# Frequency-pair layout for the scratch tensors of a two-stage transform in a gated convolution kernel

## The chip, the cores and the metric

The kernel runs on one core of a Trainium2 chip. The metric is the device time of one execution in microseconds; lower is better. A core has a matrix engine (PE, with its weight loads PEld), a vector engine (DVE), a scalar engine (ACT), a general engine (POOL) and a synchronisation engine (SP). SP issues most of the transfers between device memory (DRAM) and the on-chip memory; ACT and POOL issue some. The transfers themselves are carried out by 16 DMA engines that all issuers share.

## The reference

The input `x` has 2048 tokens of 512 channels. Two branches are mixed by a gate:

```python
g = sigmoid((x * gate_w).sum(-1))                        # one gate per token
K[d, l] = Re(sum_n C[d,n] * exp(dt[d]*A[d,n]*l) * dt[d]*B[d,n])   # 2048 taps per channel, complex A, B, C
a = irfft(rfft(pad(x)) * rfft(pad(K)))[:2048] + x * Dskip # causal convolution over the tokens
b = gelu(x @ w1 + b1) @ w2 + b2                           # 512 -> 1792 -> 512
out = g * a + (1 - g) * b
```

Everything is float32.

## The kernel before

The program has two halves in time. The function `front` runs the dense branch `b`, the making of the taps `K`, and the first stage of the transform of both `x` and `K`. The function `conv` then runs the second stage of both transforms, their product, the inverse transform, and the mix with the gate.

**The transform in two stages.** The tokens are split into 64 slots of 32 tokens. `first_stage` (L405) multiplies one slot's 32 rows by a constant matrix `c1` of 32 x 64, which gives 32 frequencies, each with a real and an imaginary part: 64 partitions, 512 channels. One call handles eight slots. Signal results are copied to on-chip tiles by ACT and stored by SP into the DRAM scratch tensor `tu_d` (L437, one store of 64 partitions and 128 KB per slot). Tap results are gathered in the tiles `sk` (two of them, each used again two calls later) and stored into `tk_d` (L802, 64 stores of 128 KB, each 64 partitions times 16 slots times 32 channels, so in pieces of 128 bytes).

Both scratch tensors have the shape [32 frequencies, 128, 512]; the 128 are the two parts times the 64 slots. So what the second stage needs of one frequency lies in one piece of 256 KB, in the order in which it stands on the 128 partitions of the chip, and the stores have the stride.

**The second stage.** `conv` walks over 16 pairs `s` of frequencies, `n = 2s` and `n = 2s+1`. Per pair, `signal(s)` and `taps(s)` multiply the loaded tiles `us[n]` and `t2s[n]` by 128 x 64 matrices (L1188), the two frequencies of the pair side by side. `product(s)` multiplies the results on DVE (L1210 to L1215), `inverse(s)` transforms back on PE (L1227), and `turn(s)` copies the two results on ACT into two of six tiles `sa` (L1239) and stores them with SP into a third scratch tensor `t4_d` (L1241). A tile `sa` is used again three pairs later, so its copy then waits until the store has landed. After the 16 pairs the last matrices (L1343) and the gate give the result.

**The loads.** The 32 tiles of the signal are loaded from `tu_d`: 27 of them by `early` in `front` (L462), as soon as rooms on the chip come free, and 5 in `conv` (L1307, for `s` of 4 to 6). The 32 tiles of the taps are loaded by `fetch` (L1167): 16 ahead of the first pair, then four in each of the pairs 0 to 3. Eight of these tiles lie in the pool `tk` and are used twice, 16 in the tile `t3`.

**The order.** In `front` the order of every instruction is a list written into the program (`ORDER`, L89), made from estimated costs and due times; it fixes the order on each engine's queue and SP's too. In `conv` the order is that of the Python loop (L1283 to L1328). SP issues its transfers strictly in that order: one that waits holds back all behind it. Completion is counted on eight semaphores that are taken in turn, and a transfer waits for the eighth transfer before it on SP, so SP has at most eight under way.

**The result.** It is kept as [16 token tiles, 128, 512]. In `front` the dense branch is written to it (L1032) and, for the second half of the hidden columns, added to it in memory from POOL (L1038). In `conv` it is read back two tiles at a time by `mix` (L1266), and stored two tiles at a time (L1362), the last two singly (L1360).

Of the kernel before, what the change touches and what calls it, by code (L numbers as in the profile page):

```python
# [9 lines left out]
F32 = mybir.dt.float32  # L10
# [4 lines left out]
ALU = mybir.AluOpType  # L15
# [3 lines left out]
P = 128  # L19
L = 2048  # L20
D = 512
# [61 lines left out]
N_ATTIC, N_LOFT, N_TK = 11, 8, 8  # L83
# [75 lines left out]
    return [32 + m if m < 32 else 63 - m for m in range(64)]  # L159


def k0_order():
    return [8 * (n % 4) + n // 4 for n in range(32)]

# [15 lines left out]
def constants():  # L180


    def om(e4):
        a = 2.0 * np.pi * (np.asarray(e4) % (4 * L)) / (4 * L)
        return np.cos(a), -np.sin(a)

    k0 = np.arange(32)
    p = np.arange(32)
    q = np.asarray(slot_q())
    k1 = np.arange(64)  # L190
    m = np.arange(32)

    er, ei = om(4 * (64 * np.outer(p, k0) + 16 * p[:, None]))

    c1 = np.tile(np.stack([er, ei], 2).reshape(32, 64), (4, 1))
    some = np.arange(P)[:, None] == np.arange(P) // 4
    c1 = np.concatenate([c1, some], 1)


    ko = np.asarray(k0_order())  # L200
    turn = 2.0 * np.pi * (ko[:, None] + 0.25) / 32
    half = 2.0 * np.pi * (ko[:, None] + 0.25) / 64
    g1 = np.zeros((P, 2, 2, 32))
    for b in range(2):
        up, down = turn * (p - 1), turn * p
        if b:
            rows = [np.cos(up), -np.sin(up), -np.sin(up), -np.cos(up)]
            rows += [np.cos(down), -np.sin(down), np.sin(down), np.cos(down)]
        else:
            z = np.zeros_like(up)  # L210
            rows = [np.cos(down), -np.sin(down), z, z]
            rows += [z, z, np.cos(up + half), -np.sin(up + half)]
        for sign in range(2):
            for kind, c in ((0, 0), (0, 1), (1, 0), (1, 1)):
                a = rows[4 * sign + 2 * kind + c] / L
                for n in range(32):
                    g1[seat(n, c, kind), b, sign] = a[n]
    g1 = g1.reshape(P, 128)


    f2 = np.zeros((32, 2, 64, 64))
    g2 = np.zeros((32, 64, 32, 2))
    for n, k in enumerate(ko):
        er, ei = om(4 * np.outer(q - 31.5, k + 32 * k1) + (q - 31.5)[:, None])
        f2[n, 0], f2[n, 1] = er, -ei
        a = 2.0 * np.pi * (k + 32 * k1 + 0.25) / L
        g2[n, :, :, 0] = np.cos(np.outer(a, m))
        g2[n, :, :, 1] = np.sin(np.outer(a, m))
        g2[n, :, 0, 1] = 1 - 2 * (k1 % 2)
    f2 = f2.reshape(8, 4, P, 64).transpose(0, 2, 1, 3).reshape(8, P, 256)  # L230
    g2 = g2.reshape(8, 2, P, 64).transpose(0, 2, 1, 3).reshape(8, P, 128)
    c2 = np.concatenate([f2, g2], 2)
    return (
        np.ascontiguousarray(c1, dtype=np.float32),
        np.ascontiguousarray(g1, dtype=np.float32),
        np.ascontiguousarray(c2, dtype=np.float32),
    )
# [38 lines left out]
def gated_mix(  # L276
# [18 lines left out]
    nc = tc.nc  # L295
# [3 lines left out]

    dt_d = dr.tile([1, D], F32, name="dt_d")  # L300
    t4_d = dr.tile([4, 2, GROUP, 2, 32, D], F32, name="t4_d")
    tu_d = dr.tile([32, P, D], F32, name="tu_d")
    tk_d = dr.tile([32, P, D], F32, name="tk_d")

    half_pi = cp.tile([P, 1], F32, name="half_pi")
    nc.vector.memset(half_pi, PI / 2)
# [22 lines left out]
    def front(pool, psum, keep, attic, loft, den, pr):  # L329
# [89 lines left out]
            for r, (bank, key) in enumerate(banks):  # L419
                evac(r, bank, key)  # L420

        rows = tu_d.rearrange("k (c t) d -> (k c) t d", c=2)

        def signal():
            for s in range(8):
# [18 lines left out]
        def early():  # L444

            us = places(attic, loft, den)
            keys = [("ux", 0)] + [("st", k) for k in range(3)]
            keys = [*keys, *(("ld", k) for k in range(N_LD)), "gwb"]
            yield 1e6
            cc, f1 = first(pr)  # L450
            move(192, lambda: nc.sync.dma_start(cc, c2[0]), T_EARLY, [], ["pr"])
            act(0.6, lambda: parted(cc, f1), T_EARLY, [], ["pr"])
            for n in range(N_US):
                m = n - N_DEN
                if m < 0:
                    due, key = T_DEN + n, [("xc", n // 4)]
                elif m < N_ATTIC:
                    due, key = T_EARLY + 2.5 * m, [keys[m]]
                else:
                    due, key = T_LOFT + m, ["xt", "xv"] if m < N_ATTIC + 4 else ["tt"]  # L460
                move(
                    256, lambda n=n: nc.sync.dma_start(us[n], tu_d[k0_order()[n]]), due,  # L462
                    [("u_d", k) for k in range(64)], key,
                )
            yield None
# [285 lines left out]
        def contract(u, c, k, t):  # L751
# [45 lines left out]
            for h in range(8):  # L797
                n, ss = h % 2, slice(h // 2 * 16, h // 2 * 16 + 16)
                d = u * UW + n * 64 + c // 2 * 32

                def store(n=n, ss=ss, d=d):
                    nc.sync.dma_start(  # L802
                        tk_d[:, :, d : d + 32].rearrange("k (c s) g -> (k c) s g", c=2)[:, ss],
                        sk[half][64 * n : 64 * n + 64, ss].rearrange("p s j g -> p s (j g)"),
                    )

                move(300, store, t + 5, [("sk", half, j) for j in range(4)], [], hold=1.4)
# [180 lines left out]
        def output(i, t):  # L988
# [18 lines left out]
            for s in range(2):  # L1007
                if b == NB - 1 and s >= 2 - N_LATE:
                    for n, f in enumerate(fs):
                        late.append((s, hi[:, n], lo[:, n], wh[1][f % FH], wl[1][f % FH]))  # L1010
                    continue
                q = (2 * b + s) % N_ACC
                n = 3 * len(fs)
                if b == NB - 2 and j == 3:
                    late.append((2 + s, hi[:, 0], lo[:, 0], wh[1][fs[0] % FH], wl[1][fs[0] % FH]))
                else:
                    mm(
                        0.2305 * n, lambda s=s, q=q: products(s, acc[q]), t + LAG + D_OUT * (j == 3),
                        [hk, lk, *ws], [("acc", q)],
                    )  # L1020
                if j == 3:
                    n = b % NSB * 2 + s
                    r = (2 * b + s) % 2
                    act(
                        0.58, lambda n=n, q=q, r=r: nc.scalar.mul(io[r], acc[q], gate[:, 1, n : n + 1]),
                        t + D_EV, [("acc", q), ("gate", b % NSB)], [("io", r)],
                    )
                    if b + 1 < NSB:
                        seed(q, t + D_EV)
                    if b < NSB:  # L1030
                        move(
                            256, lambda n=n, r=r: nc.sync.dma_start(out[n], io[r]), t,  # L1032
                            [("io", r)], [("v", n)],
                        )
                    else:
                        move(
                            512,
                            lambda n=n, r=r: nc.gpsimd.dma_start(out[n], io[r], accum_op=ALU.add),  # L1038
                            t, [("io", r)], [("v", n)], queue="GP",
                        )  # L1040

# [106 lines left out]
    def conv(pool, ps, late, attic, loft, den, pr):  # L1148
# [10 lines left out]
            nc.sync.dma_start(cc, c2[m])  # L1159
            c4s[m] = cc  # L1160

        def fetch(n):
            if N_TK <= n < N_TK + 16:
                t2s[n] = t3[:, 16 + n - N_TK if n < N_TK + 8 else n - N_TK]
            else:
                t2s[n] = pool.tile([P, D], F32, tag="tk", name=f"tk{n}", bufs=N_TK)
            nc.sync.dma_start(t2s[n], tk_d[ko[n]])  # L1167

        def matrices(m):

# [87 lines left out]
        def mix(k, on):  # L1258
# [4 lines left out]
            else:  # L1263
                r -= N_ATTIC
                mos[k] = loft[:, r * D : (r + 2) * D].rearrange("p (s d) -> p s d", s=2)
            on.dma_start(mos[k], out[2 * k : 2 * k + 2].rearrange("s p d -> p s d"))  # L1266

        def rest(n):

# [10 lines left out]
                nc.tensor.matmul(accs[s], l[:, ss], w, start=False, stop=last)  # L1280
                n -= 1

        for n in range(N_TK):  # L1283
            if n == 4:
                factors(1)
            fetch(n)
            if n == 1:
                t3 = pool.tile([P, 24, D], F32, name="t3", bufs=1)
                g1t = pool.tile([P, 2, 64], F32, name="g1t", bufs=1)
        for n in range(N_TK, N_TK + 8):  # L1290
            fetch(n)
        nc.sync.dma_start(g1t, g1.rearrange("p (b k) -> p b k", b=2))
        matrices(0)
        signal(0)
# [4 lines left out]
        for s in range(16):  # L1299

            if s % 2 or s == 0:
                if s < 10:
                    factors((s + 5) // 2)
            for n in range(16 + 4 * s, 20 + 4 * s) if s < 4 else ():
                fetch(n)
            for n in range(2 * s + N_ROOM, min(2 * s + N_ROOM + 2, 32)) if s > 3 else ():
                nc.sync.dma_start(us[n], tu_d[ko[n]])  # L1307
            product(s)
            if 1 < s + 1 < 16:
                signal(s + 1)  # L1310
# [22 lines left out]
        for m in range(8):  # L1333
            tag = "pa" if m % 3 == 2 else f"pu{m % 3}"
            for i in range(2):
# [19 lines left out]
                for h, cs in enumerate(parts):  # L1355
# [1 line left out]
                        z[:, cs], pb[:, cs], gate[:, 0, t : t + 1], z[:, cs], ALU.mult, ALU.add  # L1357
                    )
                    if m == 7:
                        (nc.sync, nc.scalar, nc.sync)[i + h].dma_start(out[t][:, cs], z[:, cs])  # L1360
            if m < 7:
                nc.sync.dma_start(out[2 * m : 2 * m + 2].rearrange("s p d -> p s d"), mos[m])  # L1362

    ctx.enter_context(tc.manual_schedule())
    keep = ctx.enter_context(tc.tile_pool(name="keep", bufs=1))
# [78 lines left out]
```

## Time and profile before

| | |
|---|---|
| Median of three runs (lowest to highest) | 492.07 us (490.47 to 492.58) |
| The profiled execution, its own time | 491.67 us |
| Its span, first to last instruction | 489.9 us |
| PE busy | 472.9 us, 97% of the span |
| DVE, ACT, POOL busy | 84%, 74%, 7% |
| Moved by DMA | 107.56 MB, mean 220 GB/s |

The profile's page lists, per engine, the time in which it was busy. "The chain that ended last" is followed back from the last instruction, at each step to what released it. The groups of transfers give the destination and source, the issuing engine, the number, the size of each and the median time from issue to landing. In the view of stages (a row per stretch of time) each engine has its busy time, followed by the clock granted to PE, the mean busy share of the 16 DMA engines and what they moved per second; the share can be a little over 1, since one engine can have two packets open. SPq and ACTq stand for the transfers that these engines issue, and the time of such a row is that of the issue.

### The profile page before, as it was taken

The numbers are of one execution on the slowest core, as the hardware profiler recorded it, in microseconds if no ns is written. First come the engines' busy times: TensorE is split into PE (matmuls) and PEld (weight loads), VectorE is DVE, ScalarE is ACT, GpSimd is POOL, SyncE is SP. The second block draws the span as 40 slices with busy tenths as digits, with TensorE's granted clock in tenths as the row PEclk, the third lists the DMA queues.
The fourth block names the chain that finished last, engine by engine and source line by source line (L and its number), as shares of the span: only waits on it lengthen the run. The fifth ranks groups of instructions, "written<-read, shape, count | busy, mean of one in ns | idle before, by whom it ended". The sixth has DMA issues, their size and how long they took to land.

```text
span 489.9 us, 11986 instructions
## 1 busy us (share of the span) xinstructions
PE 472.9 (97%) x4802; PEld 355.2 (72%) x4802; DVE 413.8 (84%) x645; ACT 363.6 (74%) x660; POOL 36.5 (7%) x63
## 2 busy tenths in 40 slices
PE   9999999997899998999999999999999999999994
PEld 7999878787688787887888878988989322222541
DVE  5879999998999999999999998999921398778355
ACT  6899895889897989999978995769754455655210
POOL 2000000000000000000011011102000100241000
PEclk8999999999899999999999999999999999999998
DMA  8868394920788458967783884884889999979897
GB/s 294 256 225 283 96 311 142 298 95 1 206 238 181 123 166 219 266 162 237 169 212 57 144 183 112 155 219 57 193 209 229 339 374 369 356 281 414 276 332 301
DMA packets 114848, 107.56 MB, mean 220 GB/s; under 512 B 72564, under 2 KB 77064, under 8 KB 114248
## 3 DMA queue, kind: packets, MB, share of 16 engines
q1 hardware_dynamic: 108072, 82.81, 57.3%
q0 software_dynamic: 6016, 20.70, 15.7%
q10 hardware_dynamic: 704, 3.28, 1.9%
q8 instruction: 38, 0.62, 0.5%
q14 instruction: 18, 0.15, 0.1%
HBM read 61.14 MB, written 45.62 MB: 218 GB/s over the span
## 4 chain that ended last, share of the span: by engine, by line
PE 80%; DVE 8%; ACT 7%; issue 2%; DMA 1%; SPq 0%; DVEq 0%; POOL 0%; POOLq 0%
PE ph L957 9%; PE ph L959 9%; PE acc L1000 9%; PE ph L958 9%; PE acc L1001 8%; PE acc L1003 8%; PE pk L761 6%; PE p2u L1188 5%; PE p2k L1188 5%; PE pa L1227 3%; PE ph L416 3%; PE pb L1343 2%; DVE loft L693 1%; DMA t<-tk_d 1%; DVE den L700 1%
## 5 line engine op out<-in xcount | busy, mean ns | idle before, releaser
L957 PE MATMUL ph<-xh,wh 128*128 128x256 f32 x448 | 128.6, 287 | 1.4 <-DVE hl L984 1.4
L959 PE MATMUL ph<-xh,wl 128*128 128x256 f32 x448 | 127.5, 285 | 0.3 <-issue 0.3
L958 PE MATMUL ph<-xlo,wh 128*128 128x256 f32 x448 | 127.4, 284 | 0.0
L957 PEld LDWEIGHTS ph<-xh,wh 128*128 128x128 f32 x448 | 85.8, 192 | 9.9 <-issue 4.1
L958 PEld LDWEIGHTS ph<-xlo,wh 128*128 128x128 f32 x448 | 85.9, 192 | 1.8
L959 PEld LDWEIGHTS ph<-xh,wl 128*128 128x128 f32 x448 | 85.9, 192 | 0.5 <-issue 0.5
L1000 PE MATMUL acc<-wh,hh 128*128 128x512 f32 x208 | 83.8, 403 | 1.0 <-ACT hh L977 0.9
L1003 PE MATMUL acc<-wh,hl 128*128 128x512 f32 x208 | 81.6, 392 | 1.9 <-DVE hl L984 1.9
L1001 PE MATMUL acc<-wl,hh 128*128 128x512 f32 x208 | 81.6, 392 | 0.0
L693 DVE TENSOR_TENSOR loft<-den,wz 128x512 f32<-128x512 f32 (+2 forms) x48 | 67.0, 1396 | 1.2 <-ACT den L675 1.1
L974 ACT ACTIVATE ph<-ph,b1t 128x256 f32<-128x256 f32 x112 | 50.5, 451 | 19.0 <-PE ph L959 17.0
L984 DVE TENSOR_TENSOR hl<-ph,hh 128x512 fp32r<-128x512 f32 (+1 forms) x62 | 38.1, 616 | 23.5 <-ACT hh L977 23.3
L1000 PEld LDWEIGHTS acc<-wh,hh 128*128 128x128 f32 x208 | 39.1, 188 | 15.8 <-issue 4.9
L1003 PEld LDWEIGHTS acc<-wh,hl 128*128 128x128 f32 x208 | 39.1, 188 | 11.7 <-DVE hl L984 3.1
L1001 PEld LDWEIGHTS acc<-wl,hh 128*128 128x128 f32 x208 | 39.1, 188 | 6.0
L1196 ACT COPY k<-p2k 128x512 f32<-128x512 f32 x32 | 18.5, 586 | 26.3 <-issue 10.2
L724 DVE TENSOR_TENSOR y<-y,ea 128x256 f32<-128x256 f32 (+2 forms) x48 | 37.1, 774 | 0.4 <-ACT y L712 0.2
L977 ACT CAST hh<-ph 128x512 fp32r<-128x512 f32 (+1 forms) x62 | 33.0, 532 | 5.9 <-PE acc L1001 1.5
L700 DVE TENSOR_TENSOR den<-loft 128x256 f32<-128x256 f32 (+2 forms) x48 | 37.1, 773 | 0.1
L761 PEld LDWEIGHTS pk<-y,den 128*32 128x32 f32 x2048 | 32.3, 112 | 6.7 <-ACT attic L434 2.8
L736 DVE TENSOR_TENSOR y<-y,loft 128x2048 f32<-128x2048 f32 x16 | 36.6, 2286 | 0.6 <-ACT loft L667 0.5
L761 PE MATMUL pk<-y,den 128*32 128x64 f32 x2048 | 35.1, 226 | 0.8 <-ACT attic L434 0.6
(194 smaller groups left out, 830.2 us busy)
## 6 DMA issues: line engine op xcount, KB each, us to landing
tk_d<-sk SPq DMA_DIRECT2D x64, 128.0 KB, 4.4
t_d<-sa SPq DMA_DIRECT2D x32, 256.0 KB, 5.0
tu_d<-attic SPq DMA_DIRECT2D x48, 128.0 KB, 3.8
attic<-in_xt_dram SPq DMA_DIRECT2D x16, 256.0 KB, 4.5
attic<-in_xs_dram SPq DMA_DIRECT2D x16, 256.0 KB, 4.7
xh_d<-xh SPq DMA_DIRECT2D x8, 512.0 KB, 5.6
xl_d<-xlo SPq DMA_DIRECT2D x8, 512.0 KB, 6.1
out_dram<-io SPq DMA_DIRECT2D x16, 256.0 KB, 3.6
```

The costliest lines, as they stand in the source:

```text
L693: v.tensor_mul(s.rearrange("p (a n l) -> p a n l", n=n, l=CL), a, w.to_broadcast([P, 4 * CH, n, CL]))
L700: v.tensor_add(to, z[:, :, 0], z[:, :, 1])
L761: nc.tensor.matmul(pks[q][32 * j : 32 * j + 32, :, gg], x[:, r, ch // CL, :, ch % CL], y[:, r, ch // CL, :, ch % CL], start=(r == 0), stop ...
L957: nc.tensor.matmul(p, h, xh[xk][:, d], start=(d == 0), stop=False)
L958: nc.tensor.matmul(p, h, xlo[xk][:, d], start=False, stop=False)
L959: nc.tensor.matmul(p, lo, xh[xk][:, d], start=False, stop=(d == 3))
L974: nc.scalar.activation(phs[q][:, n], phs[q][:, n], AF.Gelu_apprx_tanh, bias=b1t[:, f : f + 1])
L984: nc.vector.tensor_sub(lo, phs[q][:, 0:nf], hi.bitcast(F32))
L1000: nc.tensor.matmul(a, h, wh[1][w], start=start, stop=False, skip_group_check=seeded)
L1001: nc.tensor.matmul(a, h, wl[1][w], start=False, stop=False, skip_group_check=seeded)
L1003: nc.tensor.matmul(a, l, wh[1][w], start=False, stop=stop, skip_group_check=seeded)
L1188: nc.tensor.matmul(out[64 * i : 64 * i + 64], w, x, start=True, stop=True)
```

## The change

Four things change in the layout of data in DRAM. Arithmetic, the list `ORDER`, the instructions of PE, DVE and ACT stay the same.

- Both scratch tensors get the shape [64 slots, 16 pairs, 2 parts, 2 of the pair, 512], and the columns of `c1` are put in the order pair, part, member, so that the 64 partitions of a first-stage result stand in the order of the memory. A store of one slot of the signal then fills one piece of 128 KB. A store of the taps keeps its 128-byte pieces, with another stride.
- A signal load (still 256 KB, one frequency) reads its 128 rows of 2 KB through `turned`: parts outermost, then slots, 128 KB apart.
- A tap load brings both frequencies of a pair in one transfer of 512 KB, 16 in place of 32, with rows of 4 KB: again parts outermost, then slots, 128 KB apart.
- The result has the shape [8 pairs of token tiles, 128, 2, 512]; a pair of tiles is one row of 4 KB per partition. The rows that `front` writes singly are 2 KB, 4 KB apart. The host puts the result back in order, outside the measured time.

```diff
+def turned(z, n):
+    return z[:, n // 2, :, n % 2].rearrange("t c d -> c t d")
...
-    c1 = np.tile(np.stack([er, ei], 2).reshape(32, 64), (4, 1))
+    c1 = np.stack([er, ei], 1)[:, :, k0_order()].reshape(32, 2, 16, 2)
+    c1 = np.tile(c1.transpose(0, 2, 1, 3).reshape(32, 64), (4, 1))
...
-    tu_d = dr.tile([32, P, D], F32, name="tu_d")
-    tk_d = dr.tile([32, P, D], F32, name="tk_d")
+    tu_d = dr.tile([64, 16, 2, 2, D], F32, name="tu_d")
+    tk_d = dr.tile([64, 16, 2, 2, D], F32, name="tk_d")
...
-        rows = tu_d.rearrange("k (c t) d -> (k c) t d", c=2)
+        rows = tu_d.rearrange("t s c a d -> (s c a) t d")
...
-                    256, lambda n=n: nc.sync.dma_start(us[n], tu_d[k0_order()[n]]), due,
+                    256, lambda n=n: nc.sync.dma_start(us[n], turned(tu_d, n)), due,
...
-                        tk_d[:, :, d : d + 32].rearrange("k (c s) g -> (k c) s g", c=2)[:, ss],
+                        tk_d[ss, :, :, :, d : d + 32].rearrange("t s c a g -> (s c a) t g"),
...
-                            256, lambda n=n, r=r: nc.sync.dma_start(out[n], io[r]), t,
+                            256, lambda n=n, r=r: nc.sync.dma_start(out[n // 2, :, n % 2], io[r]), t,
...
-                            lambda n=n, r=r: nc.gpsimd.dma_start(out[n], io[r], accum_op=ALU.add),
+                            lambda n=n, r=r: nc.gpsimd.dma_start(out[n // 2, :, n % 2], io[r], accum_op=ALU.add),
...
-        def fetch(n):
+        def fetch(s):
+            n = 2 * s
             if N_TK <= n < N_TK + 16:
-                t2s[n] = t3[:, 16 + n - N_TK if n < N_TK + 8 else n - N_TK]
+                r = 16 + n - N_TK if n < N_TK + 8 else n - N_TK
+                t = t3[:, r : r + 2]
             else:
-                t2s[n] = pool.tile([P, D], F32, tag="tk", name=f"tk{n}", bufs=N_TK)
-            nc.sync.dma_start(t2s[n], tk_d[ko[n]])
+                t = pool.tile([P, 2, D], F32, tag="tk", name=f"tk{s}", bufs=N_TK // 2)
+            t2s[n], t2s[n + 1] = t[:, 0], t[:, 1]
+            nc.sync.dma_start(t, tk_d[:, s].rearrange("t c a d -> c t a d"))
...
-            on.dma_start(mos[k], out[2 * k : 2 * k + 2].rearrange("s p d -> p s d"))
+            on.dma_start(mos[k], out[k])
...
-            for n in range(16 + 4 * s, 20 + 4 * s) if s < 4 else ():
+            for n in range(8 + 2 * s, 10 + 2 * s) if s < 4 else ():
                 fetch(n)
...
-                nc.sync.dma_start(us[n], tu_d[ko[n]])
+                nc.sync.dma_start(us[n], turned(tu_d, n))
...
-                nc.sync.dma_start(out[2 * m : 2 * m + 2].rearrange("s p d -> p s d"), mos[m])
+                nc.sync.dma_start(out[m], mos[m])
...
-    args.append(nc.dram_tensor("out_0_dram", (16, P, D), F32, kind="ExternalOutput").ap())
+    args.append(nc.dram_tensor("out_0_dram", (8, P, 2, D), F32, kind="ExternalOutput").ap())
...
-    o = np.asarray(r.results[0]["out_0_dram"])
+    o = np.asarray(r.results[0]["out_0_dram"]).transpose(0, 2, 1, 3)
```

More of the change, by code (lines that the diff above doesn't have):

```diff
@@ L1281, in rest @@
                 n -= 1
-        for n in range(N_TK):
-            if n == 4:
+        for s in range(N_TK // 2):
+            if s == 2:
                 factors(1)
-            fetch(n)
-            if n == 1:
+            fetch(s)
+            if s == 0:
                 t3 = pool.tile([P, 24, D], F32, name="t3", bufs=1)
                 g1t = pool.tile([P, 2, 64], F32, name="g1t", bufs=1)
-        for n in range(N_TK, N_TK + 8):
-            fetch(n)
+        for s in range(N_TK // 2, N_TK // 2 + 4):
+            fetch(s)
         nc.sync.dma_start(g1t, g1.rearrange("p (b k) -> p b k", b=2))
@@ L1359, in conv @@
                     if m == 7:
-                        (nc.sync, nc.scalar, nc.sync)[i + h].dma_start(out[t][:, cs], z[:, cs])
+                        (nc.sync, nc.scalar, nc.sync)[i + h].dma_start(out[t // 2, :, t % 2, cs], z[:, cs])
             if m < 7:
-                nc.sync.dma_start(out[2 * m : 2 * m + 2].rearrange("s p d -> p s d"), mos[m])
+                nc.sync.dma_start(out[m], mos[m])
     ctx.enter_context(tc.manual_schedule())
```

## The prediction

> **What bounds the kernel now.** First the share of the chain of waits by engine on the profile's page, then that chain in order of time, near the seam between `front` and `conv` and after it. A row has start, length and what it was.
>
> ```profile
> PE 80%; DVE 8%; ACT 7%; issue 2%; DMA 1%; SPq 0%; DVEq 0%; POOL 0%; POOLq 0%
> ```
>
> ```profile
> 383.24 7.20 DMA t<-tk_d
> ...
> 392.35 1.68 PE pa L1227 x8
> ...
> 434.44 1.02 PE pa L1227 x8
> ...
> 482.78 0.74 DVE attic L1356
> ```
>
> PE sets the time, and transfers are on the path only at the seam. From the first `inverse` at 392.35 to the tenth at 434.44 a pair takes (434.44 − 392.35)/9 = 4.7 us, on PE all the way: every load is there in time. Next the groups of transfers that the change touches or that stand among them (KB each, median us from issue to landing) and SP's issues.
>
> ```profile
> t_d<-sa SPq DMA_DIRECT2D x32, 256.0 KB, 5.0
> tu_d<-attic SPq DMA_DIRECT2D x48, 128.0 KB, 3.8
> attic<-tu_d SPq DMA_DIRECT2D x16, 256.0 KB, 4.6
> tk<-tk_d SPq DMA_DIRECT2D x16, 256.0 KB, 5.3
> t<-tk_d SPq DMA_DIRECT2D x16, 256.0 KB, 6.0
> den<-tu_d SPq DMA_DIRECT2D x8, 256.0 KB, 3.6
> loft<-tu_d SPq DMA_DIRECT2D x8, 256.0 KB, 3.9
> ```
>
> ```profile
> 273.21 0.33 SPq L462 DMA_DIRECT2D attic<-tu_d  x1
> ...
> 377.19 0.43 SPq L462 DMA_DIRECT2D attic<-tu_d  x1
> 377.79 1.74 SPq L1167 DMA_DIRECT2D tk<-tk_d  x4
> ```
>
> Of the 32 signal loads 27 are issued from 273.21 to 377.19; the tap loads begin at 377.79. Last the stages: after the pairs of busy time stand PE's granted clock, the busy share of the 16 DMA engines, and GB/s.
>
> ```profile
> core 0: us, PE busy (x) PEld busy (x) DVE busy (x) ACT busy (x) POOL busy (x), PEclk, DMA share, GB/s
> 273.00:377.00 104.00, 103.11 (x1252) 90.31 (x1253) 83.32 (x117) 75.32 (x122) 11.55 (x16) 1.00 0.76 165
> 377.00:392.00 15.00, 14.47 (x82) 7.49 (x81) 5.03 (x9) 7.54 (x16) 1.75 (x2) 1.00 1.02 328
> 392.00:416.00 24.00, 23.66 (x124) 6.56 (x124) 21.48 (x37) 13.15 (x25) 0.00 (x0) 1.00 1.03 372
> 440.00:456.00 16.00, 16.00 (x88) 4.48 (x88) 12.32 (x21) 8.63 (x16) 2.01 (x3) 1.00 0.95 373
> ```
>
> So 16 engines are about full around the seam, with the work spread over all of them. What one busy engine moves follows: 373/(16 × 0.95) = 24.5 GB/s in the last row, 372/(16 × 1.03) = 22.6 in the one before, 328/(16 × 1.02) = 20.1 at the seam.
>
> **How a transfer is spread.** This is where I expect the change to be decided. Today every signal and tap load has 128 rows on both sides. Afterwards the DRAM side counts 2 parts, then 64 slots, then a row. Whether the outermost count matters can be read off the packets of the first 35 us, which begin and end with the DMA idle (queue, packets, MB, share; then all of SP's issues in that stretch):
>
> ```profile
> q1 hardware_dynamic: 5544, 9.32, 78.5%
> ...
> sk<-in_w_dram SPq DMA_DIRECT2D x8, 256.0 KB, 4.6
> attic<-in_xt_dram SPq DMA_DIRECT2D x6, 256.0 KB, 3.5
> y<-in_w_dram SPq DMA_DIRECT2D x6, 256.0 KB, 5.1
> attic<-in_xs_dram SPq DMA_DIRECT2D x6, 256.0 KB, 5.1
> xh_d<-xh SPq DMA_DIRECT2D x2, 512.0 KB, 5.1
> xl_d<-xlo SPq DMA_DIRECT2D x1, 512.0 KB, 5.3
> pr<-in_prm_dram SPq DMA_DIRECT2D x1, 384.0 KB, 6.8
> ux<-in_xl_dram SPq DMA_DIRECT2D x1, 256.0 KB
> attic<-in_xl_dram SPq DMA_DIRECT2D x1, 256.0 KB, 4.5
> ...
> b1t<-in_b_dram SPq DMA_DIRECT2D x1, 7.0 KB, 5.4
> dt_d<-dts SPq DMA_DIRECT2D x1, 2.0 KB, 2.3
> dm<-in_dskip_dram SPq DMA_DIRECT2D x1, 2.0 KB
> ```
>
> Of these 35 transfers, 33 move one piece per row of 128 rows, `pr` six per row, and `dm` (L1086) has only four rows: 33 × 128 + 768 + 4 = 4,996 pieces. The queue carried 5,544 packets, 548 more. If every transfer ended with one small packet per engine on 16 engines, that would be 35 × 16 = 560. It is 34 × 16 + 4: the one transfer with outermost count 4 reported from four engines. So I take it that a transfer is dealt out along its outermost count, that a load with an outermost 2 against 128 runs on 2 engines, and that they are the same two for each load on SP; which engines `dm` took, no row shows.
>
> The Trainium skill, page "DMA: Bandwidth & Descriptors", section "Why a DMA increments its semaphore by 16 and not by 1", says it as a rule: the number of engines is the largest up to 16 that divides the outermost sizes above 1 of both sides, and transfers issued from SP take the lowest-numbered ones. By that rule the loads run on two fixed engines and the sum below holds; the trace's 548 agrees with it, and for which engines it is the only source. It is the rule that speaks against this change, whose larger rows would otherwise only help.
>
> **The change part by part.**
>
> *The loads.* I price an engine at 24.5 GB/s, from the stretch whose share is below 1 (above 1, engines have two packets open, and the quotient is no longer the pace of one); bounds 20.1 to 24.5. A signal load puts 131,072 bytes on each of the two engines, 5.35 us; a tap load of 512 KB puts 262,144 there, 10.7 us. Before, a 256 KB load took 16,384 bytes, 0.67 us, of every engine.
>
> From 273.21 the two engines carry 27 × 5.35 = 144.5 us of signal loads. Their share of all else up to 377 is 0.76 × 104 − 27 × 0.67 = 60.9 us. That is 205 us of work in 104 us: the pair is 101 us behind at 377. Queued on SP behind these loads stand the tap stores (L802); the first tap load waits for the last of those, and comes no earlier than the pair reaches it. The stretch to 392 adds 1.02 × 15 − 16 × 0.67 = 4.6 us. The first tap load lands at 273.21 + 144.5 + 60.9 + 4.6 + 10.7 = 493.9, when before the whole span of 489.9 was over.
>
> Then pairs come at the pace of the tap loads, 10.7 us against 4.7. PE, DVE and ACT wait. Worse, SP has at most eight transfers under way, so the stores of `turn` (L1241) are held back behind the tap loads, and a tile `sa` comes free late. All 16 tap loads and the five signal loads of L1307 stand ahead of the stores of pair 6 on SP, whose landing frees the tiles for pair 9:
>
> ```profile
> 435.52 1.07 ACT L1239 COPY sa<-pa 128x512 f32<-128x512 f32 x2 [0.39 <-PE pa L1227]
> ```
>
> So that copy, at 435.52 before, follows 493.9 + 15 × 10.7 + 5 × 5.35 + 14 stores × 0.67 = 690.6. From it to the end of the span of 489.9 us were 54.4 us, which I leave as they are, since no wide load is left by then: 745.0. The profiled execution took 491.67, 1.8 more than its span: **747 us**. (That execution lies 0.4 below the median of 492.07, so the sum needs no correction.) Not counted are the constants and POOL's own loads and stores, whose share on the pair would add to it, and PE's clock after its waits. At 20.1 GB/s the 342 us of narrow loads grow by 75: 822. If on the other hand the 101 us behind at 377 were hidden (the signal loads going on beside the rest at no cost), 646.
>
> *Half as many tap issues, rows of 4 KB.* 16 issues less on SP, about 0.4 us each by the four in 1.74 us above, 7 us of SP's time. With SP held by landings this is worth nothing; if all 16 engines took part it would count at the seam alone.
>
> *The signal's stores* become one piece of DRAM, *the taps' stores* keep 65,536 pieces of 128 bytes with a stride of 128 KB instead of 2. Both are hidden: PE is busy 103.11 of 104 us in 273 to 377 with the DMA engines at 0.76. From a gain of nothing to a third more engine time (what 0.76 leaves) they stay hidden; with the cover gone, the latter would be some 20 us in that stretch. I take 0.
>
> *The result's layout* keeps 128 as the outermost count everywhere; reading and writing in rows of 4 KB is at most a small gain in the last 54.4 us, and rows of 2 KB at 4 KB distance replace a contiguous store. I take 0, bounds a microsecond each way, by the 5.35 × 2/16 = 0.67 us that such a transfer holds an engine.
>
> **The rivals.**
>
> *All 16 engines take part* (the rows on the chip's side decide): not slower. For it: `t_d<-sa` has 64 outermost against 128 and lands as fast as others, so sides may differ; but 64 still divides by 16. Then only the seam moves. DVE waited there for POOL's transfers out of `io`:
>
> ```profile
> 387.86 0.69 DVE L1210 TENSOR_TENSOR v<-p2u,k 128x512 f32<-128x512 f32 x1 [4.49 <-DMA out_dram<-io]
> ...
> 389.81 0.69 DVE L1211 TENSOR_TENSOR v<-p2u,k 128x512 f32<-128x512 f32 x1 [1.26 <-DMA out_dram<-io]
> ```
>
> Fewer packets beside these could save up to the 1.26: 490.4 to 492, so 491.
>
> *Two engines, but other ones each time.* The total per engine stays as before, and only a load's own duration grows. A first tap load would land 5.3 − 0.67 + 10.7 = 15.3 us after 377.79, at 393.1 and not at 383.1; up to 10 us are lost at the seam, the rest is prefetched: 500 us. Against it: one queue issues them all, and nothing in the trace rotates.
>
> *Rows 128 KB apart read slower still*, the 64 rows of one engine falling on the same part of memory. At half the rate the 342 us double: 1,090. Against it: `tu_d<-attic` writes 64 rows 128 KB apart today and lands in 3.8 us. The Trainium skill, same page, section "Latency and other measured facts", gives copies with 512 KiB between rows 207 GB/s, with 2 MiB 164, against 214 at full rate, and has no figure for 128 KiB; no run here shows it.
>
> **How the numbers follow.** Two fixed engines 0.84 (747 us), all 16 0.08 (491), changing pairs 0.05 (500), slow rows 0.03. The predicted time is the first. Its own bounds are 646 and 822, with the uncounted work 840: the range 640 to 840 holds about 8 in 10, since the other cases lie outside. A measurement of this kernel can tell 0.5% from no change, some 2.5 us. The chances: slower 0.92 (the first, third and fourth case), same 0.06, faster 0.02 (the best of all-16).
>
> **What would show it.** Right: signal and tap loads land tens of microseconds after their issue; the mean DMA share falls to about 2/16 plus a little from 380 on, with GB/s near 2 × 24.5 = 49; SP waits longest for `tk_d` and `tu_d` loads; pairs follow each other at about 10.7 us; the first 270 us are unchanged; 16 q1 completions less for each load that was dropped and 14 for each narrow one. Wrong: loads that land in 4 to 7 us, or a share near 1 around the seam (all 16, or changing pairs). If the loads are narrow but `front` itself ends late, past 382, then stores of `sk` held back reached ACT and PE, which I have costed at nothing.

## The result and the profile after

| | before | after |
|---|---|---|
| Median (lowest to highest), four runs each | 492.11 us (490.47 to 492.58) | 740.87 us (738.15 to 742.81) |
| The profiled execution, its own time / span | 491.67 / 489.9 us | 741.3 / 739.3 us |
| PE busy | 97% of the span | 68% |
| Mean of all DMA traffic | 220 GB/s | 145 GB/s |

The change makes the kernel slower: the ratio is 1.506 with a 95% interval of 1.502 to 1.510. The forecast was 747 us with a range of 640 to 840. Of all executions in this document one, of the kernel with bigger tap loads from rows as before, took 1,608.7 us where the others of that kernel took 491.44 to 494.39; it is left out of that kernel's median, and nothing on record explains it.

The page of after first: span, PE's busy share and the DMA engines' share in 40 slices of 18.5 us each, what they moved, the queue of SP's transfers (q1), and the shares of the chain of waits.

```profile
span 739.3 us, 11963 instructions
...
PE   9999997999999999994399111014305330436896
...
DMA  7768642855877846744461323111112112154898
GB/s 251 262 203 257 188 164 58 246 132 180 235 202 208 188 70 134 150 109 84 83 131 57 78 61 70 51 61 52 52 64 86 53 77 86 77 209 160 312 358 319
...
q1 hardware_dynamic: 104200, 82.80, 36.6%
...
PE 43%; SPq 26%; DMA 17%; ACT 7%; DVE 4%; issue 3%; ACTq 0%; DVEq 0%; POOL 0%; POOLq 0%
```

Up to slice 18 PE is as full as before. Slices 19 and 20 are thin, 21 and 22 full again, and from 23 to 35 PE mostly waits, while the DMA engines stand at a tenth to three tenths of their capacity and move 51 to 86 GB/s. A kernel that waits for transfers while the DMA engines look almost idle is the picture of a few busy engines among sixteen. PE's share of the chain fell from 80% to 43%; SP's issues (SPq, 26%) and the landings (DMA, 17%) took 43%.

The stages by time (columns as in the view of stages before):

```profile
273.00:377.00 104.00, 79.67 (x956) 69.09 (x956) 76.02 (x109) 63.07 (x100) 9.74 (x14) 0.89 0.55 117
...
480.00:520.00 40.00, 12.85 (x40) 3.16 (x40) 10.51 (x17) 5.40 (x10) 0.00 (x0) 0.66 0.14 56
520.00:560.00 40.00, 6.23 (x24) 1.55 (x24) 4.41 (x8) 2.24 (x4) 0.00 (x0) 0.60 0.15 58
...
700.00:740.00 40.00, 32.81 (x160) 15.85 (x156) 21.28 (x33) 5.66 (x10) 0.51 (x1) 0.95 0.89 334
```

From 480 to 560 the share is 0.14 to 0.15 of 16 engines, so 2.2 to 2.4 of them, and 56/2.2 = 25 GB/s for each. Three to four tap loads were under way at the time: when SP began the fifth at 498.35 (its rows follow below), one had landed. Had they been on different pairs of engines, several pairs would have worked side by side. PE's granted clock falls with its work, from 1.00 in the stages of before to 0.60.

PE's waits for taps, from its timeline (start, length, instruction, in brackets the idle time before it and what ended it):

```profile
490.97 3.33 PE L1197 MATMUL p2k<-tk,pr 128*64 128x512 f32 x8 [38.43 <-DMA tk<-tk_d]
501.09 3.39 PE L1197 MATMUL p2k<-tk,pr 128*64 128x512 f32 x8 [6.79 <-DMA tk<-tk_d]
511.63 1.98 PE L1197 MATMUL p2k<-tk,cc 128*64 128x512 f32 x4 [7.15 <-DMA tk<-tk_d]
521.67 1.97 PE L1197 MATMUL p2k<-tk,cc 128*64 128x512 f32 x4 [3.90 <-DMA tk<-tk_d]
...
562.62 1.97 PE L1197 MATMUL p2k<-t,cc 128*64 128x512 f32 x4 [34.72 <-DMA cc<-in_c_dram]
```

The first taps are there at 490.97, where the forecast had 493.9. Before, the same matrix product (then L1188) began at 385.42:

```profile
385.42 3.68 PE L1188 MATMUL p2k<-tk,pr 128*64 128x512 f32 x16
```

The next three follow at (521.67 − 490.97)/3 = 10.2 us. A tap load puts 262,144 bytes on an engine, so one busy engine moves 25.6 GB/s, a little more than the 24.5 of the forecast. Then comes something the forecast had not counted: PE waits 34.72 us for `cc`, the constants of the next two pairs (L1165, 192 KB from device memory). SP's rows, with start and length of each group of issues, show where they stood:

```profile
487.37 10.74 SPq L1176 DMA_DIRECT2D tk<-tk_d  x2
498.35 33.30 SPq L1176 DMA_DIRECT2D t<-tk_d  x4
531.69 16.79 SPq L1301 DMA_DIRECT2D g1t<-in_g_dram  x1
548.52 1.06 SPq L1165 DMA_DIRECT2D cc<-in_c_dram  x1
```

Before, four issues of tap loads took 1.74 us together. Now one lasts nearly as long as a narrow load takes. The length of a single issue (minimum, median and maximum in ns), first before and then after:

```profile
L1167 SPq DMA_DIRECT2D t<-tk_d x16: 319/326/1737, 383.2 to 399.3; - x16
```

```profile
L1176 SPq DMA_DIRECT2D t<-tk_d x8: 542/8808/9831, 498.3 to 571.8; - x8
```

This is not the hold that the forecast named, a wait for the eighth transfer before. By SP's timeline its issues themselves fill 212 of the 218 us from 466.69 to 685.08, and only one of its waits there, of 3.9 us, is ended by a landing. What makes an issue last so long, no run here shows. So SP comes to the constants at 548.52, 20.6 us after PE began to wait for them. They then land 14 us after their issue (the median before was 5.0); they spread over all 16 engines, two of which have a queue of tap loads.

The copies of `turn` on ACT (L1248, before L1239) for pairs 4, 5, 9 and 10, counted from 0:

```profile
605.22 1.22 ACT L1248 COPY sa<-pa 128x512 f32<-128x512 f32 x2 [16.30 <-DMA t_d<-sa]
626.65 1.22 ACT L1248 COPY sa<-pa 128x512 f32<-128x512 f32 x2 [19.24 <-DMA t_d<-sa]
...
685.41 1.22 ACT L1248 COPY sa<-pa 128x512 f32<-128x512 f32 x2 [4.26 <-DMA t_d<-sa]
689.69 1.07 ACT L1248 COPY sa<-pa 128x512 f32<-128x512 f32 x2 [0.39 <-PE pa L1236]
```

The copy of pair 9 starts at 685.41 (before 435.52), the pairs behind it run at PE's pace again, and from it to the end are 739.3 − 685.41 = 53.9 us (before 54.4). So the whole loss, 249.4 us of the span, lies before that copy. The copy is 249.9 us late: 490.97 − 385.42 = 105.6 until the first taps, 144.3 between them and pair 9.

### The profile page after: what moved, and what is told of

It is laid out like the page before. It is cut to its first block, busy times and chain, and to the rows that moved or that the text cites. A ratio compares the mean times of both kernels' runs of the same rounds, so it can differ in the third digit from the quotient of the medians.

```text
span 739.3 us, 11963 instructions
## 1 busy us (share of the span) xinstructions
PE 501.6 (68%) x4802; PEld 362.1 (49%) x4802; DVE 414.8 (56%) x645; ACT 363.9 (49%) x660; POOL 34.8 (5%) x63
## 3 DMA queue, kind: packets, MB, share of 16 engines
q1 hardware_dynamic: 104200, 82.80, 36.6%
## 4 chain that ended last, share of the span: by engine, by line
PE 43%; SPq 26%; DMA 17%; ACT 7%; DVE 4%; issue 3%; ACTq 0%; DVEq 0%; POOL 0%; POOLq 0%
DMA t_d<-sa 9%; SPq L808 8%; SPq L1176 7%; DMA cc<-in_c_dram 7%; SPq L468 6%; PE ph L963 6%; PE ph L965 5%; PE ph L964 5%; PE acc L1006 5%; PE acc L1007 5%; PE acc L1009 5%; PE pk L767 3%; SPq L1301 2%; PE ph L422 2%; PE p2k L1197 2%
## 5 line engine op out<-in xcount | busy, mean ns | idle before, releaser
L1219 DVE TENSOR_TENSOR v<-p2u,k 128x512 f32<-128x512 f32 x16 | 11.1, 691 | 238.0 <-ACT k L1205 90.0
L1205 ACT COPY k<-p2k 128x512 f32<-128x512 f32 x32 | 18.5, 588 | 119.8 <-PE p2k L1197 102.3
L1248 ACT COPY sa<-pa 128x512 f32<-128x512 f32 x32 | 17.9, 587 | 98.3 <-DMA t_d<-sa 91.2
L1197 PE MATMUL p2k<-t,cc 128*64 128x512 f32 x32 | 12.0, 836 | 75.7 <-DMA cc<-in_c_dram 75.7
L1197 PEld LDWEIGHTS p2k<-t,cc 128*64 128x64 f32 x32 | 2.4, 171 | 81.7 <-ACT sa L1248 44.2
L1236 PE MATMUL pa<-v,cc 64*64 64x512 f32 x112 | 20.3, 737 | 27.8 <-ACT sa L1248 27.8
```

## The experiments

The kernels below are the kernel before or after with one edit each. In the texts that were written ahead of the runs, "halves" means that a load of 128 partitions is issued as two loads of 64 partitions, one for each part, so that 64 slots are the outermost count.

**Halves for both, and for one of the two.** The layout stays that of after; the loads no longer have an outermost 2.

```diff
+def parts_two(on, to, z):
+    for c in range(2):
+        on.dma_start(to[64 * c : 64 * c + 64], z[c])
...
-    lambda n=n: nc.sync.dma_start(us[n], turned(tu_d, n)), due,
+    lambda n=n: parts_two(nc.sync, us[n], [tu_d[:, n // 2, c, n % 2] for c in range(2)]), due,
...
-            nc.sync.dma_start(t, tk_d[:, s].rearrange("t c a d -> c t a d"))
+            parts_two(nc.sync, t, [tk_d[:, s, c] for c in range(2)])
```

With both edits (and the same at L1316):

> The changed kernel with each signal and tap load as two transfers of 64 partitions, one per part, whose outermost count is the 64 slots on both sides. Layout in memory, rows 128 KB apart and bytes stay as in the changed kernel. Theory (an outermost count of 2 leaves two fixed engines): all 16 engines take part again, pairs at 4.7 us, 490 to 500 us; the surplus over 492 would be the seam, where SP issues twice as many loads and eight under way are half as many bytes. Rival (rows 128 KB apart are what is slow): it stays above 600 us.

Measured: 503.71 us, ratio 1.024 (1.019 to 1.028), so 3.7 us above the expected range. The first taps are there at 393.97, which is 8.6 us later than before: most of the surplus lies at the seam. With halves for the signal alone, so that only the tap loads stay narrow:

> Only the signal loads in two transfers of 64 partitions; the tap loads stay with an outermost 2. Theory: the two engines are free until the tap loads start at about 378, the first lands at 378 + 4.6 + 10.7 = 393, 15 more at 10.7 us, then stores and signal loads of 0.67 us each: the stores of pair 6 land at about 566, 54.4 us to the end and 1.8 around the span: 622 us (610 to 640). If the loss were in the signal loads, about 500; if it were spread evenly over all bytes, half of it, about 616, with pairs that are not at 10.7 us.

Measured: 636.32 us, ratio 1.294 (1.288 to 1.299), in the expected range, though the first taps came at 402.66 and not at 393. With halves for the taps alone, so that only the signal loads stay narrow:

> Only the tap loads in two transfers of 64 partitions; the signal loads stay with an outermost 2. Theory: the pair of engines is 101 us behind at 377, the first tap load lands at about 483 in place of 383, then pairs run at 4.7 us, since the five late signal loads are asked for eight pairs ahead: 492 + 100 = 592 us (575 to 605).

Measured: 614.15 us, ratio 1.249 (1.244 to 1.253), above what was expected.

Of the 249 us, 237 go with the outermost 2. The narrow signal loads cost about 122 alone and the narrow tap loads 144 alone; both figures are against the kernel before, so they hold what the halves of the other loads cost. The kernel with narrow signal loads also measures a step of the forecast by itself. PE's first taps there:

```profile
485.40 5.12 PE L1203 MATMUL p2k<-tk,pr 128*64 128x512 f32 x16 [34.28 <-DMA tk<-tk_d]
```

485.40 − 385.42 = 100 us: the two engines were forecast to be 101 behind at 377. The other 22 are what I had called hidden in the expectation: the five late signal loads, behind which stores of `turn` stand. ACT's copies, pairs 6 to 9 of the same kernel:

```profile
523.22 1.07 ACT L1254 COPY sa<-pa 128x512 f32<-128x512 f32 x2 [0.39 <-PE pa L1242]
540.57 1.22 ACT L1254 COPY sa<-pa 128x512 f32<-128x512 f32 x2 [13.13 <-DMA t_d<-sa]
552.73 1.20 ACT L1254 COPY sa<-pa 128x512 f32<-128x512 f32 x2 [6.70 <-DMA t_d<-sa]
559.16 1.22 ACT L1254 COPY sa<-pa 128x512 f32<-128x512 f32 x2 [4.26 <-DMA t_d<-sa]
```

The three steps take 35.9 us. At the pace of the kernel before, 4.6 to 4.7 a pair, they would take 14: 22 us, the rest of the 122.

**The outermost count alone.** The kernel before, with one row of 2 KB left unused after each G-th part of the 128 rows of a frequency. The stores write the same pieces, moved by the unused rows. Rows stay next to each other, but a load now counts G parts on the DRAM side, then 128/G rows. The result lies as before.

```diff
+def spread(z, k):
+    return z[k, :, :, 0 : 128 // G].rearrange("c h t d -> (c h) t d")
...
-    tu_d = dr.tile([32, P, D], F32, name="tu_d")
-    tk_d = dr.tile([32, P, D], F32, name="tk_d")
+    tu_d = dr.tile([32, 2, G // 2, 128 // G + 1, D], F32, name="tu_d")
+    tk_d = dr.tile([32, 2, G // 2, 128 // G + 1, D], F32, name="tk_d")
...
-            nc.sync.dma_start(t2s[n], tk_d[ko[n]])
+            nc.sync.dma_start(t2s[n], spread(tk_d, ko[n]))
```

> The kernel before, with one unused row of 2 KB between the two parts of a frequency in both scratch tensors, so that a load counts 2 parts, then 64 adjacent rows; 32 tap loads of 256 KB as before. Nothing else of the change. Theory: two engines again, 5.35 us for each load, two tap loads a pair: the same sum as for the change, 740 us (720 to 760). Rival (rows 128 KB apart, or rows of 4 KB, are what is slow): 492 us.

> The kernel before, with one unused row of 2 KB after every 32 slots in both scratch tensors: a load counts 4 outermost, then 32 adjacent rows. Theory: four engines, 2.68 us a load on each. Four engines are 29 us behind at 377; then 273.2 + 72.2 + 60.9 + 4.6 + 85.6 + 13.4 + 9.4 = 519 for the stores of pair 6, and 54.4 + 1.8: 576 us (560 to 590). Rival (any break in the rows costs the same): as with 2 outermost, 745.

> The kernel before, with one unused row after every 16 slots: a load counts 8 outermost. Theory: eight engines, 1.34 us a load on each; they are not behind at 377, and a pair needs 2.7 us of them for its taps, below the 4.7 of PE; only around the seam, where all engines were full, the eight carry some 14 us more than before: 495 to 510 us. Rival as above: 745.

| outermost count of a load | first taps on PE | time | ratio (95%) |
|---|---|---|---|
| 128 (before) | 385.42 | 491.7 to 492.1 | 1 |
| 8 | 396.03 | 519.55 | 1.056 (1.053 to 1.058) |
| 4 | 419.08 | 588.96 | 1.197 (1.193 to 1.200) |
| 2 | 483.45 | 745.38 | 1.515 (1.509 to 1.522) |
| 2, rows 128 KB apart (after) | 490.97 | 740.87 | 1.506 (1.502 to 1.510) |

Each halving of the count costs more than the one before. With 2 and adjacent rows the time is that of after within 0.7%, so no price of the distance of 128 KB shows. (The kernel with 2 also has 32 tap loads of 256 KB, where after has 16 of 512 KB.) The packets agree too: SP's queue on the pages of before and of the kernels with 2, 4 and 8:

```profile
q1 hardware_dynamic: 108072, 82.81, 57.3%
```

```profile
q1 hardware_dynamic: 107176, 82.80, 37.1%
```

```profile
q1 hardware_dynamic: 107304, 82.80, 46.9%
```

```profile
q1 hardware_dynamic: 107560, 82.80, 53.9%
```

896, 768 and 512 packets are missing: 64 loads times 14, 12 and 8, one completion packet for each engine that takes no part. This is the rule of the Trainium skill, page "DMA: Bandwidth & Descriptors", section "Why a DMA increments its semaphore by 16 and not by 1", that the largest number up to 16 that divides the outermost sizes is the number of engines; the trace agrees for 2, 4 and 8.

For 2 the time lies in the expected range, for 4 at its upper end, and for 8 it is 10 us above, since I had worked out the narrow loads' own time and left out who stands behind them. In the kernel with 8 the first taps are 10.6 us late, but ACT's copy for pair 9 is 26.5 late (462.06 against 435.52). On the way PE waits 4.85 us for the constants of pair 2, and landings of `turn`'s stores end waits of ACT. ACT's copies for pairs 7, 8 and 9:

```profile
447.65 1.20 ACT L1246 COPY sa<-pa 128x512 f32<-128x512 f32 x2 [1.67 <-DMA t_d<-sa]
459.34 0.59 ACT L1246 COPY sa<-pa 128x512 f32<-128x512 f32 x1 [7.59 <-DMA t_d<-sa]
...
462.06 0.59 ACT L1246 COPY sa<-pa 128x512 f32<-128x512 f32 x1 [0.28 <-PE pa L1234]
```

**The rest of the change without the narrow loads.** First the result's layout alone, on the kernel before (the stores of `front` change with it, as in the change).

```diff
-            on.dma_start(mos[k], out[2 * k : 2 * k + 2].rearrange("s p d -> p s d"))
+            on.dma_start(mos[k], out[k])
...
-                nc.sync.dma_start(out[2 * m : 2 * m + 2].rearrange("s p d -> p s d"), mos[m])
+                nc.sync.dma_start(out[m], mos[m])
```

> The kernel before with only the result in pairs of token tiles (rows of 4 KB for reads and stores in the last part, rows of 2 KB 4 KB apart for the stores of the first). Theory: no load on the path moves: 492 within 1 us. Rival (the accumulating stores that the first product waits for get slower with the distance): up to 3 us more.

Measured: 491.89 us, ratio 1.000 (0.999 to 1.002). Then with it half as many tap loads of 512 KB, from scratch that has the shape of before with the frequencies in the order of the pairs, so that 128 stays outermost:

```diff
-    c1 = np.tile(np.stack([er, ei], 2).reshape(32, 64), (4, 1))
+    c1 = np.tile(np.stack([er, ei], 2)[:, k0_order()].reshape(32, 64), (4, 1))
...
-            nc.sync.dma_start(t2s[n], tk_d[ko[n]])
+            nc.sync.dma_start(t, tk_d[n : n + 2].rearrange("a p d -> p a d"))
```

> The kernel before with the scratch by frequency and rows adjacent as before, the frequencies in the order of use, so that a tap load of 512 KB brings a pair with 128 rows outermost, two pieces of 2 KB each; the result in pairs of token tiles as in the change. So half as many tap loads on SP, all on 16 engines. Theory: the same as before, 490.5 to 493, since a tap load is not on the path after the seam; at best 1.3 us less at the seam. Rival (larger loads hold up the first pair, which needs only 512 KB): 2 to 5 us more.

Measured: 492.74 us, ratio 1.002 (1.001 to 1.004). The bigger tap loads bring no gain that shows, even where all 16 engines carry them. Their pieces in DRAM are still of 2 KB, two for each partition and 256 KB apart, so this kernel doesn't test rows of 4 KB. No version tried is faster than the kernel before.

**Where the remaining 12 us of the halves come from.** That last kernel with both loads in halves, so 64-partition loads from adjacent rows:

```diff
-            nc.sync.dma_start(t, tk_d[n : n + 2].rearrange("a p d -> p a d"))
+            parts_two(nc.sync, t, tk_d[n : n + 2].rearrange("a p d -> p a d"))
```

> The kernel with rows adjacent and a pair per tap load (the result in pairs too), with each signal and tap load as two transfers of 64 partitions: number, size and order of the transfers on SP are those of the changed kernel with halved loads (503.7 us); only the rows lie 2 KB apart and not 128 KB. If the 11.6 us that kernel lost came from halved loads (half the partitions at a time, half the bytes under way): again 502 to 505. If they came from the distance of 128 KB between rows: 492 to 494.

Measured: 508.36 us, ratio 1.034 (1.031 to 1.038), above both bands. The distance of 128 KB is gone and the loss is not, so it belongs to the halved loads. It even grew by 4.7 us. The expectation left out one difference: a tap load has two pieces of 2 KB for each partition here and one of 4 KB in the layout of after (107,688 against 105,640 packets on SP's queue). The stage 392 to 416, of the kernel with halves in the layout of after, then of this one:

```profile
392.00:416.00 24.00, 20.06 (x82) 5.21 (x84) 14.57 (x24) 9.79 (x19) 0.00 (x0) 0.79 1.04 268
```

```profile
392.00:416.00 24.00, 19.12 (x88) 5.20 (x90) 14.89 (x25) 10.61 (x20) 0.00 (x0) 0.90 1.07 249
```

The engines are as busy as before (1.03 there) and move 268 and 249 GB/s in place of 372, though not the same mix of transfers. Whether that lies in the 64 partitions of the chip's side, in twice as many transfers, or in both, these runs don't separate.

**Who holds the pairs back after the first taps?** The forecast said that stores of `turn` stand behind narrow loads among the eight transfers under way on SP, and that the late tiles `sa` hold ACT. SP's rows of after already speak against the eight. Three runs took the rest apart. First the stores issued by ACT.

```diff
-                nc.sync.dma_start(t4_d[g, :, k].rearrange("e c q d -> (c q) e d"), sa)
+                nc.scalar.dma_start(t4_d[g, :, k].rearrange("e c q d -> (c q) e d"), sa)
```

> The changed kernel with the stores of turn issued by ACT in place of SP, so that they no longer stand behind the tap loads. Step under test: the tiles sa come free late because those stores are held on SP. Theory: the loads stay narrow, so the first tap and the pace of the loads stay; but turn no longer waits, and the end follows the last signal load (about 680) by 36 us and 1.8: 718 to 733 us. If the hold on SP is not what sets the last part, 741.

Measured: 752.73 us, ratio 1.531 (1.527 to 1.535): slower than after, against my theory, and above the 741 us of the other one. ACT's timeline:

```profile
604.66 0.59 ACT L1248 COPY sa<-pa 128x512 f32<-128x512 f32 x1 [0.65 <-ACT sa L1248]
655.11 0.53 ACTq L1250 DMA_DIRECT2D t_d<-sa  x1
655.73 1.07 ACT L1205 COPY k<-p2k 128x512 f32<-128x512 f32 x2 [50.48 <-DMA tk<-tk_d]
```

ACT waits 50 us to issue one store, and what ends its wait is the landing of a tap load that SP issued. The store needs nothing of that load. So SP's and ACT's transfers count on the same eight semaphores, and here that limit does hold: ACT's own work stood behind it. Next the stores on POOL (the same line with `nc.gpsimd`), whose transfers count on others:

> The kernel after, with the stores of turn issued by POOL, whose queue has semaphores of its own and issues nothing else between 408 and 650 us. If the stores of the first pairs are late because SP's and ACT's transfers share eight semaphores (so that a store waits until the eighth transfer before it has landed), they now go out at once, the tiles sa come free early, and the last part starts with the last tap and signal loads: 16 tap loads at 10.2 us from 491 and five signal loads at 5.1 end at about 670, and some 45 to 55 us stand behind that: 715 to 730. If instead the stores, of which two sixteenths lie on the two busy engines, wait there behind the wide rows whoever issues them, the copies into sa are as late as before: 738 to 745.

Measured: 758.56 us, ratio 1.541 (1.532 to 1.550), in neither band. No copy into `sa` waits for a store any more, and still it is slower than after. PE waits for constants instead. Those of the line below stood on SP behind two signal loads whose issues took 23.35 us, and SP came to them at 657.27:

```profile
678.47 1.97 PE L1197 MATMUL p2k<-t,cc 128*64 128x512 f32 x4 [28.88 <-DMA cc<-in_c_dram]
```

Last, stores and constants both on POOL (that line and L1165 with `nc.gpsimd`):

> The kernel after, with both the stores of turn and the loads of the constants cc issued by POOL, so that on SP only the narrow loads are left between 466 and 690 us. With the stores alone on POOL, ACT no longer waited for a store (none of its copies into sa did), but each second pair waited for its constants, which stood on SP behind narrow loads, and the time rose to 758.6. If the narrow loads' own time on two engines sets the end, and stores and constants only stand in their queue, the last of the 16 tap and five signal loads now lands at about 491 + 15 x 10.2 + 5 x 5.1 = 670, pairs follow the loads at 10.2 us, and with the 45 to 55 us behind the last of them it takes 710 to 730. If constants and stores are not the cause either, and the order of pairs and rooms (a late signal load waits for a room that a pair frees) sets the end, it stays at 738 to 760.

Measured: 750.88 us, ratio 1.528 (1.521 to 1.536). I had expected 710 to 730. The number lies in the other theory's band, but the trace speaks for neither as written. Among the pairs PE now waits for narrow loads alone. Its waits for the taps of pairs 2, 3 and 13, then for the last signal loads:

```profile
511.64 1.98 PE L1197 MATMUL p2k<-tk,cc 128*64 128x512 f32 x4 [6.68 <-DMA tk<-tk_d]
522.14 1.98 PE L1197 MATMUL p2k<-tk,cc 128*64 128x512 f32 x4 [4.16 <-DMA tk<-tk_d]
...
658.83 1.98 PE L1197 MATMUL p2k<-tk,cc 128*64 128x512 f32 x4 [5.67 <-DMA tk<-tk_d]
686.83 1.11 PE L1197 MATMUL p2u<-attic,cc 128*64 128x512 f32 x1 [22.73 <-DMA attic<-tu_d]
...
713.83 1.12 PE L1197 MATMUL p2u<-attic,cc 128*64 128x512 f32 x1 [4.32 <-DMA attic<-tu_d]
```

Where the loads are alone they come at 10.5 us; the ten from 522.14 to 658.83 take 13.7 each. The DMA queues in the window from 522 to 659 (packets, MB, share of 16 engines' time; q0 is POOL's):

```profile
q0 software_dynamic: 3107, 13.37, 29.3%
q1 hardware_dynamic: 1446, 5.32, 9.8%
```

Two engines that do nothing but SP's loads would be 2/16 = 12.5%. The loads got 9.8%, which is 78% of the two engines' time, and POOL's transfers, if spread evenly, take 29.3% of it. Together that is 107%: by this estimate the two are full, and no wait of SP for a free room leaves them idle. If POOL's transfers leave 70.7% of the two engines to the narrow loads, a load takes 10.2/0.707 = 14.4 us, against 13.7 measured. The same holds for the last stretch, from 659 to 714, though SP waits there up to 17.8 us for a free room. Of the 5.94 MB moved in it, 3.30 are SP's, and without the 1.05 of its two loads from `t4_d` some 2.25 are narrow loads, which is 44 us at 2 × 25.6 GB/s; a sixteenth of the rest is 9 us at 25.6: 53 of 55 us. So neither the order nor the issuer of the other transfers gets around it. They go through the same two engines and take time there from the narrow loads. The expected 710 to 730 left that time out. The Trainium skill, page "DMA: Bandwidth & Descriptors", section "Rules for kernel authors", says the same, that spreading transfers over issuers brings no bandwidth since all run on the same 16 engines; these three runs agree.

## Why the prediction was right

**The spread along the outermost count, on two fixed engines: right.** Time, share and packets all follow the count. In after the queue has 108,072 − 104,200 = 3,872 packets less. 2,048 are tap pieces (16 loads of 128 rows fewer) and 896 pieces of the result (seven stores of two tiles, 128 rows instead of 256 each). The other 928 are the forecast's 16 × 16 + 48 × 14 completions exactly. That the two engines are the same ones follows from the share of 0.14 with three to four tap loads under way, and from the narrow loads' falling behind at all.

**The price of an engine: 24.5 forecast, 25.6 measured,** 10.2 us a tap load in place of 10.7.

**101 us behind at 377, first taps at 493.9: right,** 100 in the run with narrow signal loads, 490.97 in after. The sum of the work fits too. From 273 to 491 the mean share of the 16 engines was 0.39, which is 85 us of each. At the measured price 27 signal loads and the first tap load are 27 × 5.12 + 10.24 = 148.5 us on each of the two engines, 18.6 in the mean of 16. The other 66 us lie on every engine, so the two had about 215 us of work in 218.

**Pairs at the pace of the tap loads, 10.7: only for the first three steps.** Then waits for constants (PE, 34.72 us) and for stores (ACT, 19.24 us) break it up.

**The stores held behind eight: held, but not by the eight, and not the cause.** ACT did wait for landings of stores, as the forecast said. Two things in that step failed. SP did not wait for the eighth transfer before; its issues themselves lasted, 212 of 218 us, so the sign that it would wait longest for `tk_d` and `tu_d` loads did not come. And the hold does not set the end: with it gone (stores on POOL) the time rose. What sets the end is the work on the two engines, the narrow loads and their sixteenth of all else; holds only choose which transfer is late. The forecast's sum worked because its 16 tap loads, five signal loads and 14 stores are most of that work. From the first taps to pair 9's copy it had 690.6 − 493.9 = 196.7 us, and 194.4 were measured. That they lie so close is in part luck. At the measured price the same terms make 15 × 10.2 + 5 × 5.1 + 14 × 0.64 = 187.5. Against that, the traffic that it named and did not count is real: from 491 to 685 the queues moved 17.4 MB, of which these 20 narrow loads are 9.2. A sixteenth of the other 8.2 MB is 20 us at 25.6 GB/s, where the 14 stores make 9. That gives an estimated 199 us of work on each of the two engines in 194 us. A price too high and work left out stood against each other.

**The front costed at nothing: wrong by itself, without effect on the sum.** `front` did end late, as the forecast's last sentence allowed:

```profile
362.53 0.58 ACT L795 COPY sk<-ph 128x512 f32<-128x512 f32 x1 [23.76 <-DMA tk_d<-sk]
```

ACT waited 23.76 us for a tile `sk` whose stores stood behind signal loads, and PE had 79.67 of 104 us in place of 103.11. By the 215 of 218 us above the two engines were busy all that time, and the first taps waited for them anyway, so next to nothing was added.

**The 54.4 us to the end: right,** 53.9 were measured. **Result layout and half the issues at nothing: right,** by the two runs without narrow loads (ratios 1.000 and 1.002). For tap rows of 4 KB no run on 16 engines without halves shows it. With halves, the kernel that has them took 503.71 us and the one with pieces of 2 KB 508.36.

**The rivals.** All 16 engines (491) and changing pairs (500) fell with the first profile, by tap loads 10.2 us apart at a share of 0.14. Rows 128 KB apart (1,090): the kernel with adjacent rows takes 745.38 against 740.87, so no such price shows. The Trainium skill, page "DMA: Bandwidth & Descriptors", section "Latency and other measured facts", has losses for wider distances between rows; at 128 KB none shows here.

## What to carry to other kernels

Before a layout is changed, write down the outermost count of each transfer's access on both sides: loads of 128 partitions read as 2 times 64 went through two of 16 engines here and cost half the kernel's time again. A low mean DMA share next to PE's waits for loads is the mark of it, and the packets of the queue count the engines. Work out the load of the busiest engine, other transfers' shares included, and don't expect a rearranged order or another issuer to mend it.

## What was not expected of the hardware

- The issue of a narrow load lasted on SP nearly as long as the load itself: 8.8 us in the median for the eight tap loads into `t3` (at most 9.8), where an issue took 0.33 before, with only three to four tap loads under way. What stood behind it on SP, narrow or not, waited.
- With loads in two halves of 64 partitions each, the stage 392 to 416 moved 249 to 268 GB/s where 372 were moved before, at about the same share of busy time (503.71 and 508.36 us for the kernels).
- In this program the semaphores that limit the transfers under way are shared by SP and ACT: a store on ACT waited 50 us for a landing of one of SP's loads, and ACT's copies waited with it.
- Loads of 512 KB, in two pieces of 2 KB for each partition, in place of two loads of 256 KB were worth nothing: 492.74 us against 491.73.
